# Key and value caches of two heads loaded and worked on as one pair: 64 partitions and 128 rows a head in place of 128 partitions and 64 rows

## The chip, the cores and the metric

The kernel runs on one core of a Trainium2 chip. The metric is the device time of one execution in microseconds (us). TensorE (PE in the profile) does the matrix products, VectorE (DVE) elementwise work and reductions, ScalarE (ACT) the exponentials, GpSimd (POOL) further elementwise work, and SyncE (SP) issues the DMA transfers that bring data from HBM into SBUF.

## The reference

Four layers follow one another on a batch of two single tokens: attention with a cache, a gated MLP, and both again with the same weights and the same caches. All data are float32.

```python
B, Sq, D = 2, 1, 576;  H, Sk, Dh = 32, 8192, 128;  Df = 4608

def _A_ref(x, k_cache, v_cache, wq, wo):              # caches: (B, H, Sk, Dh)
    q = (x @ wq).reshape(B, Sq, H, Dh).transpose(0, 2, 1, 3)
    scores = jnp.einsum("bhqd,bhkd->bhqk", q, k_cache) * (Dh ** -0.5)
    p = _softmax(scores, axis=-1)
    o = jnp.einsum("bhqk,bhkd->bhqd", p, v_cache)
    return o.transpose(0, 2, 1, 3).reshape(B, Sq, H * Dh) @ wo

def _B_ref(x, w_gate, w_up, w_down):
    g, u = x @ w_gate, x @ w_up
    return (_gelu(g) * u) @ w_down

x = A_x
for _ in range(2):
    x = x + _A_ref(_layernorm(x), A_k_cache, A_v_cache, A_wq, A_wo)
    x = x + _B_ref(_layernorm(x), B_w_gate, B_w_up, B_w_down)
```

The keys of one head and one batch entry are 8192 x 128 floats, 4 MiB, and so are its values. There are 64 such heads (32 heads, two batch entries), so one attention reads 512 MiB of caches, and there are two.

## The kernel before

**Caches in SBUF.** A head's 4 MiB lie on 128 partitions: partition p holds 64 consecutive rows of 512 B, so one DMA has 128 runs of 32 KB. A tile called space takes nearly all of SBUF. It is divided into six slots of one head each (8192 floats a partition); the last slot overlaps a ring of four smaller places for weights. A class Arena keeps account, while the program is written, of which stretch is in use and when each slot was last freed. Loads stand in one queue in program order. The head of the queue is written out as a DMA on SP as soon as the account has room for it (pump); whatever frees a stretch calls done, which calls pump. On the chip, SP waits in that same order for the last reader of the room that a load overwrites, and then issues it. So one load that waits holds up all that stand behind it on SP. Most heads load as one transfer (cache); some, at the seams between layers, in quarters of 1 MiB (cache_quarter).

**Order of the loads.** In an attention the keys of head n are followed by the values of head n - 1, then the keys of head n + 1, and so on. At the end of the first attention two key caches and three value caches stay in SBUF. The second attention walks the heads backward and begins with them.

**Work on one head.** For each quarter k of the keys, multiply(n, k) has VectorE multiply the quarter by the query, in place (L461), and GpSimd add the upper half of each product row to the lower half (L465). add_up(n, k) has VectorE sum what is left (L470) and frees the quarter. The query comes broadcast over the partitions from a small matrix product (query, L445). peak and highest find the largest score (L484, L490), softmax takes the exponentials on ScalarE into prz (L496, L499), total makes the sum of the weights (L505, L509). values(n) has TensorE multiply weights and values, 16 products of four rows each (L521), and frees each quarter of the values. gather, context and divide bring the result into place for wo (L537, L546, L551). project multiplies by wo (L563).

**Order of the work.** Each engine works in the order of the program. The steps of neighbouring heads interleave: in the step of head n, the values of head n - 1 are worked on. Two lines of that step matter below:

```python
multiply(n, 0)
if before:
    add_up(n - 1, 3)
    peak(n - 1)
```

The last sum of head n - 1 stands, on VectorE, behind the first multiply of head n. The step then goes on with multiply(n, 1), highest and softmax of n - 1, add_up(n, 0), multiply(n, 2), total, values of n - 1, and the remaining quarters.

**Layers.** plan_attention and plan_mlp queue the loads of both attentions and both MLPs; attention and mlp write the work.

Of the kernel before, what the change touches and what calls it, by code (L numbers as in the profile page):

```python
# [16 lines left out]
B = 2  # L17
# [7 lines left out]
J = SK // P  # L25
NHB = H * B
JC = 16

# [9 lines left out]
SLOT = J * DH  # L38
PART = JC * DH
NSLOT = 6  # L40
# [4 lines left out]
HELD = 5  # L45


class Arena:
# [18 lines left out]
    def slot(self, key, allowed):  # L67

        for s in sorted(allowed, key=lambda s: self.freed[s]):
            if self.clear(s * SLOT, SLOT):  # L70
                return [self.take((key, k), s * SLOT + k * PART, PART) for k in range(4)]
        return None
# [23 lines left out]
def decode_layers(ctx, tc, x_in, kc, vc, wq, wo, wg, wu, wd, out):  # L96
# [36 lines left out]
    def cache_rows(at, hb, src, lo, hi):  # L133

        t = part_at(at, (hi - lo) * DH).rearrange("p (j d) -> p j d", d=DH)
        nc.sync.dma_start(t, src[hb % B, hb // B].rearrange("(p j) d -> p j d", p=P)[:, lo:hi, :])

    def quarter(at):
        return part_at(at, PART).rearrange("p (j d) -> p j d", d=DH)

    def cache(key, src, hb, allowed, pieces=1):

        def make():
            at = arena.slot(key, allowed)
            if at is None:
                return False
            for lo in range(0, J, J // pieces):
                cache_rows(at[0] + lo * DH, hb, src, lo, lo + J // pieces)
            ready[key] = [quarter(a) for a in at]
            places[key] = at  # L150
            return True

        queue.append(make)

    def cache_quarter(key, src, hb, k, where):

        def make():
            if where == "ring":
                at = arena.ring((key, k), PART)
            else:  # L160
                at = arena.take((key, k), places[where][k], PART)
            if at is None:
                return False
            cache_rows(at, hb, src, k * JC, (k + 1) * JC)
            ready.setdefault(key, {})[k] = quarter(at)
            return True

        queue.append(make)
# [58 lines left out]
    def products():  # L227

        def make():
            at = [RING + k * PLACE for k in (2, 3)]  # L230
            if not all(arena.clear(a, PLACE) for a in at):
                return False
            ready["products"] = [quarter(arena.take(("products", k), at[k], PART)) for k in range(2)]
            return True

        queue.append(make)
# [19 lines left out]
    every, front = range(NSLOT), range(HELD)  # L256

    keys_held, values_held = range(NHB - 2, NHB), range(NHB - 3, NHB)

# [3 lines left out]
    def plan_attention(layer, seq):  # L263
        for us in WQ[layer]:

            half_rows(("wq", layer, us[0]), wq, us, None if layer else 3 * SLOT)

        def keys(n):
            hb = seq[n]
            held = hb in keys_held  # L270
            if layer == 1 and held:
                return
            key = ("k", 1 if held else layer, hb)


            if layer and n == 4:
                for turn, k in (("k", 0), ("v", 0), ("v", 1), ("k", 1), ("v", 2), ("v", 3), ("k", 2), ("k", 3)):
                    if turn == "k":
                        cache_quarter(key, kc, hb, k, ("k", 1, seq[1]))
                    else:  # L280
                        cache_quarter(("v", 1, seq[3]), vc, seq[3], k, ("v", 1, seq[0]))
            elif layer and n in (2, 3, 5):
                for k in range(4):
                    cache_quarter(key, kc, hb, k, {2: "ring", 3: ("k", 1, seq[0]), 5: ("v", 1, seq[1])}[n])
            else:

                cache(key, kc, hb, every if layer or n < NHB - 3 else front)

        def vals(n):
            hb = seq[n]  # L290
            held = hb in values_held
            if not (layer == 1 and (held or n == 3)):
                allowed = every if layer or n < NHB - 4 else front
                cache(("v", 1 if held else layer, hb), vc, hb, allowed, 4 if n == NHB - 1 else 1)

        for n in range(NHB + 1):
            if n < NHB - 1:
                keys(n)
            if n == NHB - 2:
                keys(n + 1)  # L300
            if n == NHB:

                if layer == 0:
                    products()
                for g in groups(layer)[:2]:
                    out_rows(layer, g)
            if n > 0:
                vals(n - 1)
        for g in groups(layer)[2:]:
            out_rows(layer, g)  # L310
# [16 lines left out]
    forward = list(range(NHB))  # L327
    backward = forward[::-1]
    plan_attention(0, forward)
    plan_mlp(0)  # L330
    plan_attention(1, backward)
# [6 lines left out]
    ones = consts.tile([P, P], F32, name="ones")  # L338
    nc.vector.memset(ones, 1.0)
# [16 lines left out]
    prz = consts.tile([P, 3, 2 * J + 4], F32, name="prz")  # L356
    nc.vector.memset(prz, 0.0)

# [60 lines left out]
    def attention(layer, seq):  # L419
# [15 lines left out]
        po = psum1.tile([P, GH, B], F32, name="po")  # L435

        oT = once.tile([P, H // GH, GH, 2, B], F32, name="oT", tag="part")

        def query(n):

            h, b = divmod(seq[n], B)
            c, s = (h // 4) % 4, h // 16
            r = s * B + b
            qb[n] = psum2.tile([P, DH], F32, name="qp")
            nc.tensor.matmul(  # L445
                qb[n], pick[32 * c:32 * c + 4, r:r + 1].to_broadcast([4, P]),
                qsb[32 * c:32 * c + 4, (h % 4) * DH:(h % 4 + 1) * DH], start=True, stop=True,
            )

        def multiply(n, k):  # L450

            hb = seq[n]
            held = hb in keys_held
            t = ready["k", 1 if held else layer, hb][k]
            if k == 0:
                S[n] = work.tile([P, J], F32, name="S")
            u = t
            if held and layer == 0:

                u = ready["products"][k % 2]  # L460
# [6 lines left out]
        def add_up(n, k):  # L467
            hb = seq[n]
            held = hb in keys_held
# [3 lines left out]
            if held and layer == 0:  # L473
                if n == NHB - 1 and k >= 2:
                    done(("products", k - 2))
                return
            key = ("k", 1 if held else layer, hb)
            done((key, k))
            if k == J // JC - 1:
                ready.pop(key)  # L480

        def peak(n):
            m = work.tile([P, 1], F32, name="m")
            nc.vector.reduce_max(m, S[n], axis=AX.X)  # L484
# [3 lines left out]
        def highest(n):  # L488
            m1 = work.tile([1, 1], F32, name="m1")
            nc.vector.reduce_max(m1, mT.pop(n), axis=AX.X)  # L490
            mT[n] = psum2.tile([P, 1], F32, name="nb", tag="small")
            nc.tensor.matmul(mT[n], ones[0:1, :], m1, start=True, stop=True)  # L492

        def softmax(n):
            nbs = work.tile([P, 1], F32, name="nbs")
            nc.scalar.mul(nbs, mT.pop(n), -scale)  # L496
            rs[n] = work.tile([P, 1], F32, name="rs")
            pr = prz[:, n % 3, 4:].rearrange("p (g e) -> p g e", e=8)[:, :, 0:4]
            nc.scalar.activation(  # L499
                pr, S.pop(n).rearrange("p (g r) -> p g r", r=4), AF.Exp, bias=nbs, scale=scale, accum_out=rs[n],  # L500
            )

        def total(n):
            tot = psum2.tile([P, 1], F32, name="tot", tag="small")
            nc.tensor.matmul(tot, ones, rs.pop(n), start=True, stop=True)  # L505
            if n % B == 0:
                rinv[n // B] = work.tile([P, B], F32, name="rinv", bufs=4)
            b = seq[n] % B
            nc.vector.reciprocal(rinv[n // B][:, b:b + 1], tot)  # L509

        def values(n):

            hb = seq[n]
            held = hb in values_held
            key = ("v", 1 if held else layer, hb)
            t = ready[key]
            left = not (held and layer == 0)
            for g in range(J // 4):
                c = g % 4
                at = 8 * g + 4 - 4 * (hb % B)  # L520
                nc.tensor.matmul(  # L521
                    acc[32 * c:32 * c + 8, (n // B) % 2, :], prz[:, n % 3, at:at + 8],
                    t[g // 4][:, g % 4 * 4:g % 4 * 4 + 4, :].rearrange("p j d -> p (j d)"),
                    start=(n % B == 0 and g < 4), stop=(n % B == B - 1 and g >= J // 4 - 4),
# [6 lines left out]
        def gather(a):  # L531

            t = osb[a] = work.tile([P, DH], F32, name="osb")
            q = acc[:, a % 2, :].rearrange("p (r d) -> p r d", r=4)
# [6 lines left out]
        def context(a):  # L541

            lo = 32 * (seq[B * a] // B % GH)
            t = osb.pop(a)
# [3 lines left out]
        def divide(a):  # L548
            h = seq[B * a] // B
            lo = 32 * (h % GH)  # L550
            nc.vector.tensor_tensor(  # L551
                out=oT[lo:lo + 32, h // GH, :, :, :],
                in0=po[lo:lo + 32, :, :].unsqueeze(2).to_broadcast([32, GH, 2, B]),
# [184 lines left out]
```

## Time and profile before

| | us |
|---|---|
| median of 3 runs | 2709.51 (2707.89 to 2710.16) |
| the profiled execution | 2710.29 |
| its span, first to last instruction | 2708.4 |
| DVE busy in it | 1889.6 |
| POOL busy | 1208.8 |
| PE busy | 1136.5 |
| ACT busy | 84.7 |

DMA moved 1155.48 MB, a mean of 427 GB/s. Of the 244 whole cache transfers, 122 are keys and 122 values; 28 more have 1 MiB.

How to read the profile: engines are PE (products) and PEld (loading of weights), DVE, ACT, POOL and SP; "SPq" is SP's instruction queue. L461 is line 461 of the kernel. A row of a timeline has start, duration, engine, line, operation, result <- inputs, shapes, count, and in brackets the idle time before it with what ended it. A row of waits has who waited for whom, the total in us, the number of times and the longest. A row of the chain has start, duration and what it was; for a DMA, from its issue to its landing. A row of a window has the stretch, its length, busy time with number of instructions for PE, PEld, DVE, ACT and POOL, the granted clock of TensorE, the busy share of the 16 DMA engines and GB/s.

### The profile page before, as it was taken

The numbers are of one execution on the slowest core, as the hardware profiler recorded it, in microseconds if no ns is written. First come the engines' busy times: TensorE is split into PE (matmuls) and PEld (weight loads), VectorE is DVE, ScalarE is ACT, GpSimd is POOL, SyncE is SP. The second block draws the span as 40 slices with busy tenths as digits, with TensorE's granted clock in tenths as the row PEclk, the third lists the DMA queues.
The fourth block names the chain that finished last, engine by engine and source line by source line (L and its number), as shares of the span: only waits on it lengthen the run. The fifth ranks groups of instructions, "written<-read, shape, count | busy, mean of one in ns | idle before, by whom it ended". The sixth has DMA issues, their size and how long they took to land.

```text
span 2708.4 us, 19293 instructions
## 1 busy us (share of the span) xinstructions
PE 1136.5 (42%) x7320; PEld 401.7 (15%) x7320; DVE 1889.6 (70%) x1807; ACT 84.7 (3%) x399; POOL 1208.8 (45%) x522
## 2 busy tenths in 40 slices
PE   2344434343434344344644434443434343444345
PEld 0111111111111111111211111111111111111122
DVE  5777777777777777776039977777777777777740
ACT  0000000000000000000000000000000000000000
POOL 2545444444544454544016554544444444445420
PEclk8666666666666666666666766566665666666678
DMA  9999999999999999999999999999999999999998
GB/s 418 433 432 430 431 433 432 430 431 432 431 431 431 432 430 432 431 431 421 397 374 419 431 431 431 432 431 430 431 431 432 432 430 430 432 430 432 430 428 378
DMA packets 50379, 1155.48 MB, mean 427 GB/s; under 512 B 5848, under 2 KB 5872, under 8 KB 7408
## 3 DMA queue, kind: packets, MB, share of 16 engines
q1 hardware_dynamic: 50248, 1154.25, 99.6%
q8 instruction: 58, 0.95, 0.1%
q14 instruction: 33, 0.27, 0.0%
q10 hardware_dynamic: 40, 0.01, 0.0%
HBM read 1154.23 MB, written 0.00 MB: 426 GB/s over the span
## 4 chain that ended last, share of the span: by engine, by line
DMA 78%; DVE 11%; PE 8%; issue 2%; POOL 0%; another core or an unknown queue 0%; SPq 0%; ACT 0%; DVEq 0%; POOLq 0%; ACTq 0%
DMA space<-in_A_k_cache_dram 45%; DMA space<-in_A_v_cache_dram 23%; PE acc L521 7%; DVE space L461 6%; DVE S L470 3%; DMA space<-in_A_wo_dram 3%; DMA space<-in_B_w_up_dram 3%; DMA space<-in_B_w_down_dram 2%; DMA space<-in_A_wq_dram 1%; DVE osb L537 1%; PE acc L426 0%; DMA space<-in_B_w_gate_dram 0%; POOL space L465 0%; PE acc L646 0%; DVE m L490 0%
## 5 line engine op out<-in xcount | busy, mean ns | idle before, releaser
L465 POOL TENSOR_TENSOR space<-space 128x1024 f32<-128x1024 f32 x512 | 1205.9, 2356 | 1255.6 <-DVE space L461 1221.6
L461 DVE TENSOR_TENSOR space<-space,qp 128x2048 f32<-128x2048 f32 x512 | 1164.9, 2275 | 479.8 <-DMA space<-in_A_k_cache_dram 457.3
L521 PE MATMUL acc<-space,prz 128*8 128x512 f32 x4096 | 723.8, 870 | 291.8 <-DVE osb L537 170.8
L470 DVE TENSOR_REDUCE S<-space 128x16 f32<-128x1024 f32 x512 | 616.0, 1203 | 3.3 <-POOL space L465 3.3
L486 PE MATMUL mT<-ident,m 128*1 128x128 f32 x128 | 46.9, 366 | 794.1 <-DVE m L484 794.1
L521 PEld LDWEIGHTS acc<-space,prz 128*8 128x8 f32 x4096 | 133.1, 115 | 769.7 <-issue 720.9
L492 PE MATMUL nb<-m,ones 1*128 1x1 f32 x256 | 74.1, 356 | 252.9 <-DVE m L490 252.9
L486 PEld LDWEIGHTS mT<-ident,m 128*1 128x1 f32 x128 | 10.2, 79 | 819.9 <-DVE m L484 813.9
L505 PE MATMUL tot<-rs,ones 128*128 128x1 f32 x256 | 74.6, 361 | 92.8 <-ACT prz L499 92.8
L492 PEld LDWEIGHTS nb<-m,ones 1*128 1x128 f32 x256 | 63.2, 305 | 289.7 <-DVE m L490 289.7
L496 ACT ACTIVATE nbs<-nb 128x1 f32<-128x1 f32 x128 | 21.9, 171 | 2357.8 <-PE nb L492 2357.8
L551 DVE TENSOR_TENSOR oT<-po,rinv 32x16 f32<-32x16 f32 x64 | 10.9, 170 | 112.2 <-PE po L546 112.2
L505 PEld LDWEIGHTS tot<-rs,ones 128*128 128x128 f32 x256 | 63.6, 309 | 104.0 <-ACT prz L499 103.5
L412 POOL TENSOR_TENSOR rstd<-ve,mhalf 128x1 f32<-128x1 f32 x4 | 2.2, 550 | 170.9 <-DVE ve L410 170.9
L445 PE MATMUL qp<-qsb,pick 4*128 4x128 f32 x256 | 62.3, 325 | 28.5 <-DVE space L461 25.4
L537 DVE SCALAR_TENSOR_TENSOR osb<-acc,diag,osb 128x128 f32<-128x128 f32 x192 | 67.3, 351 | 6.8
L671 DVE STREAM_TRANSPOSE o<-o 128x288 f32<-128x288 f32 x4 | 2.8, 691 | 93.1 <-ACT o L669 93.1
L445 PEld LDWEIGHTS qp<-qsb,pick 4*128 4x128 f32 x256 | 38.0, 186 | 88.9 <-PE acc L521 48.1
L416 DVE TENSOR_TENSOR x<-xps,x 128x144 f32<-128x144 f32 x4 | 1.2, 307 | 71.3 <-PE xps L695 41.5
L546 PEld LDWEIGHTS po<-of,osb 128*32 128x32 f32 x512 | 40.1, 152 | 49.4 <-issue 40.8
L499 ACT ACTIVATE prz<-S,nbs 128x64 f32<-128x64 f32 x128 | 44.5, 348 | 4.5 <-ACT nbs L496 0.4
L546 PE MATMUL po<-of,osb 128*32 128x2 f32 x512 | 37.6, 195 | 6.6 <-DVE osb L537 6.6
(56 smaller groups left out, 344.6 us busy)
## 6 DMA issues: line engine op xcount, KB each, us to landing
space<-in_A_k_cache_dram SPq DMA_DIRECT2D x122, 4096.0 KB
space<-in_A_v_cache_dram SPq DMA_DIRECT2D x122, 4096.0 KB
space<-in_A_wo_dram SPq DMA_DIRECT2D x16, 1152.0 KB
space<-in_A_k_cache_dram SPq DMA_DIRECT2D x16, 1024.0 KB
space<-in_A_v_cache_dram SPq DMA_DIRECT2D x12, 1024.0 KB
space<-in_B_w_down_dram SPq DMA_DIRECT2D x9, 1152.0 KB
space<-in_B_w_gate_dram SPq DMA_DIRECT2D x3, 3456.0 KB
space<-in_A_wq_dram SPq DMA_DIRECT2D x3, 3072.0 KB
```

The lines of the kernel that those rows point to most:

```text
L445: nc.tensor.matmul(qb[n], pick[32 * c:32 * c + 4, r:r + 1].to_broadcast([4, P]), qsb[32 * c:32 * c + 4, (h % 4) * DH:(h % 4 + 1) * DH], st ...
L461: nc.vector.tensor_tensor(out=u, in0=t, in1=qb[n].unsqueeze(1).to_broadcast([P, JC, DH]), op=ALU.mult)
L465: nc.gpsimd.tensor_tensor(out=half, in0=half, in1=u[:, :, DH // 2:], op=ALU.add)
L470: nc.vector.tensor_reduce(out=S[n][:, k * JC:(k + 1) * JC], in_=prod.pop((n, k)), axis=AX.X, op=ALU.add)
L486: nc.tensor.transpose(mT[n], m, ident)
L492: nc.tensor.matmul(mT[n], ones[0:1, :], m1, start=True, stop=True)
L496: nc.scalar.mul(nbs, mT.pop(n), -scale)
L499: nc.scalar.activation(pr, S.pop(n).rearrange("p (g r) -> p g r", r=4), AF.Exp, bias=nbs, scale=scale, accum_out=rs[n],)
L505: nc.tensor.matmul(tot, ones, rs.pop(n), start=True, stop=True)
L521: nc.tensor.matmul(acc[32 * c:32 * c + 8, (n // B) % 2, :], prz[:, n % 3, at:at + 8], t[g // 4][:, g % 4 * 4:g % 4 * 4 + 4, :].rearrange(" ...
L537: nc.vector.scalar_tensor_tensor(t, q[:, r, :], diag[:, r:r + 1], t, op0=ALU.mult, op1=ALU.add,)
L546: nc.tensor.matmul(po[lo:lo + 32, i, :], t[:, i::GH], of, start=True, stop=True)
```

## The change

The heads 0 to 29 are taken in pairs: heads h and h + 1 of one batch entry, which lie side by side in HBM, are one item. Head h takes partitions 0 to 63 and head h + 1 partitions 64 to 127, with 128 consecutive rows each: one run of 64 KB a partition, 8 MiB an item, eight parts where a head had four quarters. There are 30 pairs, and four single heads (h = 30 and 31) at the end, laid out as before. A whole pair takes two neighbouring slots of the six.

In the first attention the slots of each load are written out by hand; in the second, pair takes the two neighbouring slots that have been free longest. A few pairs at the seams load in halves or single parts. A pair has two query products, two exponentials and two divisions, since its heads lie on different partitions; value products have the weights of both heads side by side. All eight wo loads of the second attention are queued behind the last values (before, two stood ahead of them). The held caches are those of the same heads as before.

```diff
+class Item:
+    def __init__(self, b, h, heads):
+        self.b, self.h, self.heads = b, h, heads
+        self.rows = SK * heads // P
+        self.parts = self.rows // JC
+
+    def source(self, cache):
+        return cache[self.b, self.h:self.h + self.heads].rearrange("h (q j) d -> (h q) j d", j=self.rows)
+
+ITEMS = [Item(b, h, 2) for h in range(0, H - 2, 2) for b in range(B)]
+PAIRS = len(ITEMS)
+ITEMS += [Item(b, h, 1) for h in range(H - 2, H) for b in range(B)]
...
+    def pair(self, key):
+        for s in sorted(range(0, NSLOT, 2), key=lambda s: max(self.freed[s:s + 2])):
+            at = self.slots(key, (s, s + 1), 8)
+            if at is not None:
+                return at
         return None
...
+    def plan_first():
...
+        for us in WQ[0]:
+            half_rows(("wq", 0, us[0]), wq, us, END - NU * H * DH // 2)
+        last = PAIRS - 1
+        at = [(2 * (i % 3), 2 * (i % 3) + 1) for i in range(2 * PAIRS)]
+        k(0, at[0])
+        for n in range(1, PAIRS):
+            k(n, at[2 * n - 1])
+            v(n - 1, at[2 * n])
+        k(SINGLE[0], (4,))
+        half(("v", 0, last), vc, last, 0, 5)
+        half(("v", 0, last), vc, last, 4, 1)
+        k(SINGLE[1], (3,))
+        v(SINGLE[0], (4,))
+        k(SINGLE[2], (0,))
+        k(SINGLE[3], (2,))
+        v(SINGLE[1], (4,))
+        v(SINGLE[2], (1,))
+        products()
+        for g in groups(0)[:2]:
+            out_rows(0, g)
+        v(SINGLE[3], (3,), (1,) * 4)
...
+    def plan_second():
...
+        for k in range(4):
+            one(("k", 1, last), kc, last, 4 + k, (v62, k))
+        half(("k", 1, last - 1), kc, last - 1, 0, 5)
+        half(("k", 1, last - 1), kc, last - 1, 4, 4)
+        cache(("v", 1, last), vc, last)
+        for n in range(last - 2, -1, -1):
+            cache(("k", 1, n), kc, n)
+            cache(("v", 1, n + 1), vc, n + 1)
+        cache(("v", 1, 0), vc, 0, None, (4, 2, 1, 1))
+        for g in groups(1):
+            out_rows(1, g)
...
         def query(n):
...
+            for i in range(it.heads):
+                h, to = it.h + i, slice(i * HALF, i * HALF + P // it.heads)
...
         def softmax(n):
...
+            for i in range(it.heads):
+                at = slice(i * HALF, i * HALF + P // it.heads)
+                nc.scalar.mul(nbs[at], nb[at, i:i + 1], -scale)
...
+        for i, n in enumerate(seq):
...
+            v = {N - 2: None, N - 1: N - 3}.get(i, i - 1) if layer == 0 else i - 1
...
+            for k in range(ITEMS[n].parts):
+                multiply(n, k)
+                if k == 0 and p is not None:
+                    add_up(p, ITEMS[p].parts - 1)
+                    peak(p)
+                if k == (0 if soon else 1) and p is not None:
+                    highest(p)
+                    softmax(p)
+                if k == 2:
+                    if p is not None:
+                        total(p)
+                    if a is not None:
+                        gather(a)
+                        if p < PAIRS:
+                            context(a)
+                    if v is not None and v >= 0:
+                        values(v)
+                    if a is not None and p >= PAIRS:
+                        context(a)
+                if k > 0:
+                    add_up(n, k - 1)
+                if k == 3 and a is not None:
+                    divide(a)
```

More of the change, by code (lines that the diff above doesn't have):

```diff
@@ L65, in take, with slots @@
         return lo
[L67 to L71, printed above, removed]
+    def slots(self, key, at, parts, first=0):
+        if not all(self.clear(s * SLOT, SLOT) for s in at):
+            return None
+        return [self.take((key, first + k), at[k // 4] * SLOT + k % 4 * PART, PART) for k in range(parts)]
+    def pair(self, key):
[3 more added lines that the diff above has]
+                return at
         return None
@@ L232, in make @@
                 return False
-            ready["products"] = [quarter(arena.take(("products", k), at[k], PART)) for k in range(2)]
+            ready["products"] = [part(arena.take(("products", k), at[k], PART)) for k in range(2)]
             return True
@@ L488, in highest @@
         def highest(n):
[L489 to L492, printed above, removed]
+            heads = ITEMS[n].heads
+            m1 = work.tile([1, 2], F32, name="m1")
+            nc.vector.reduce_max(m1[:, :heads], mT.pop(n).rearrange("p (i q) -> p i q", i=heads), axis=AX.X)
+            mT[n] = psum2.tile([P, 2], F32, name="nb", tag="small")
@@ L516, in values, with accumulator, completes @@
+        of_head = {}
+        def accumulator(n):
+            return acc[:, n % 2 if n < PAIRS else (n - PAIRS) // B, :]
+        def completes(i):
+            return seq[i] < PAIRS or i > 0 and ITEMS[seq[i - 1]].h == ITEMS[seq[i]].h
+        def values(i):
+            n = seq[i]
+            it, key, pr = ITEMS[n], name("v", layer, n), weights_of(n)
             t = ready[key]
-            left = not (held and layer == 0)
-            for g in range(J // 4):
+            left = not (layer == 0 and n in VALUES_HELD)
+            gs = it.rows // 4
+            begins = n < PAIRS or not completes(i)
+            for g in range(gs):
@@ L607, in attention, with finish @@
-        add_up(last, 3)
-        first, second, *others = groups(layer)
-        values(last - 1)
-        peak(last)
-        highest(last)
-        softmax(last)
-        project(first)
-        total(last)
-        gather(H - 2)
-        context(H - 2)
-        divide(H - 2)
-        project(second)
-        values(last)
-        gather(H - 1)
-        context(H - 1)
-        divide(H - 1)
-        for g in others:
+        def finish(n):
+            gather(n)
+            context(n)
+            divide(n)
@@ new lines, in attention @@
+        n, p = seq[-1], seq[-2]
+        add_up(n, ITEMS[n].parts - 1)
+        first, second = groups(layer)[:2]
+        if layer == 0:
+            values(N - 2)
+        peak(n)
+        highest(n)
+        softmax(n)
+        if layer == 0:
+            project(first)
+        total(n)
+        finish(seq[-3] if layer == 0 else p)
+        if layer == 0:
+            project(second)
+        values(N - 1)
+        finish(n)
+        for g in groups(layer)[2:] if layer == 0 else groups(layer):
```

305 lines of the change are left out of this document (144 added, 161 removed).

## The prediction

> **What bounds the kernel now.** I read the page first: shares, traffic by slice, queues, the chain that ended last.
>
> ```profile
> span 2708.4 us, 19293 instructions
> ...
> PE 1136.5 (42%) x7320; PEld 401.7 (15%) x7320; DVE 1889.6 (70%) x1807; ACT 84.7 (3%) x399; POOL 1208.8 (45%) x522
> ...
> GB/s 418 433 432 430 431 433 432 430 431 432 431 431 431 432 430 432 431 431 421 397 374 419 431 431 431 432 431 430 431 431 432 432 430 430 432 430 432 430 428 378
> ...
> q1 hardware_dynamic: 50248, 1154.25, 99.6%
> ...
> DMA 78%; DVE 11%; PE 8%; issue 2%; POOL 0%; another core or an unknown queue 0%; SPq 0%; ACT 0%; DVEq 0%; POOLq 0%; ACTq 0%
> ```
>
> No compute engine is over 70% busy, and SP's one queue holds the 16 DMA engines for 99.6% of the span. The slices of the two attentions run level at 430 to 433 GB/s; only the MLP in the middle and the end dip. Then the stretches by window and the waits.
>
> ```profile
> core 0: us, PE busy (x) PEld busy (x) DVE busy (x) ACT busy (x) POOL busy (x), PEclk, DMA share, GB/s
> 300.00:500.00 200.00, 77.77 (x431) 27.24 (x431) 150.67 (x140) 6.11 (x30) 96.57 (x41) 0.63 1.00 431
> ...
> 1350.00:1370.00 20.00, 10.51 (x212) 5.65 (x216) 1.84 (x7) 0.97 (x3) 0.00 (x0) 0.81 1.01 420
> ...
> 1700.00:2500.00 800.00, 326.65 (x1767) 112.92 (x1767) 598.78 (x555) 25.10 (x123) 386.29 (x164) 0.63 1.00 431
> ```
> ```profile
> DVE space L461 <- DMA space<-in_A_k_cache_dram: 457.3, 115, 14.2
> ```
>
> The DMA share in either attention is 1.00, while DVE stands still 457.3 us for keys. So the time is bytes over rate plus the time in which the DMA queue is empty, and that is next to nothing today. The bytes do not change. The change can therefore act in two ways: on the rate, and on whether the queue always has a transfer waiting.
>
> **The change, first the rate.** In layer 0, 30 key and 29 value pairs move whole as 8 MiB; in layer 1, 28 and 29: 116 transfers. Each replaces two of 4 MiB, and its 128 runs of 64 KB replace 256 of 32 KB. At 431 GB/s an engine gets 26.9 GB/s, and a 32 KB run takes 1216 ns. The 1350 to 1370 row is w_down with runs of 9 KB, engines as busy, at 420: 351 ns for 9216 B. A line through both gives about 12 ns fixed per run. Each engine saves 116 x 128 / 16 = 928 such costs: 11 us. If the engine cuts 64 KB into two, nothing is saved but some completion marks; and since both rates are rounded, I take 9 us and keep 0 to 12. On the other side, the two heads of a pair lie 4 MiB apart and neighbouring partitions 64 KB: no row shows a rate at such a spacing, so a loss is not excluded (a rival below).
>
> [...]
>
> **Then the queue in layer 0.** This is the term that decides. The room for caches becomes three places of 8 MiB, and layer 0 writes the places out by hand: load number i goes to place i mod 3, in the order K0, K1, V0, K2, V1, K3, V2 ... So V(n) overwrites K(n), and the load directly ahead of V(n) in the queue is K(n+1). When is K(n) done with? Its last part's add_up stands, in DVE's order, behind the first multiply of item n+1, which waits for K(n+1) to land. That order exists already, and the timeline shows it:
>
> ```profile
> 298.74 2.29 DVE L461 TENSOR_TENSOR space<-space,qp 128x2048 f32<-128x2048 f32 x1 [2.35 <-DMA space<-in_A_k_cache_dram]
> 300.94 1.21 DVE L470 TENSOR_REDUCE S<-space 128x16 f32<-128x1024 f32 x1
> ...
> 302.18 0.33 SPq L136 DMA_DIRECT2D space<-in_A_v_cache_dram  x1
> ```
> ```profile
> 302.18 45.11 DMA space<-in_A_v_cache_dram
> ```
> ```profile
> SPq L136 <- DVE m L484: 799.1, 122, 19.3
> ```
>
> The multiply starts as the keys land, the previous item's sum follows, and 302.18 - 298.74 = 3.44 us after the landing SP issues the next load. SP's wait list has this release 122 times. Today it costs nothing: with six places the transfer issued at 302.18 lands 45.11 us later, so over four transfers of 9.73 us lie in the queue. After the change nothing lies there: K(n+1) has landed, V(n) is the head of SP's queue and waits, and K(n+2) waits behind it in order. The DMA engines stand still from the landing until V(n)'s first bytes, in every pair.
>
> The price of one such stop. The 3.44 us are sure. After the issue there is a restart, which this profile shows where layer 1 begins with an empty queue:
>
> ```profile
> 1409.38 14.62 SPq L136 DMA_DIRECT2D space<-in_A_k_cache_dram  x5
> ```
> ```profile
> 1409.00:1410.00 1.00, 0.00 (x0) 0.00 (x0) 1.00 (x2) 0.00 (x0) 1.00 (x1) 0.50 0.00 0
> 1410.00:1411.00 1.00, 0.00 (x0) 0.00 (x0) 1.00 (x1) 0.00 (x0) 0.41 (x1) 0.50 0.86 139
> 1411.00:1412.00 1.00, 0.00 (x0) 0.00 (x0) 1.00 (x2) 0.00 (x0) 0.37 (x1) 0.50 0.81 319
> ```
>
> Against 431 GB/s that loses 0.62 us before 1410, 0.68 in the next us and 0.26 in the one after: 1.6 us from issue to full rate. Ahead of the 3.44 us is a landing's own lag, from the engines' last bytes to the waiting instruction. The end of the kernel bounds it:
>
> ```profile
> 2704.00:2705.00 1.00, 0.61 (x16) 0.33 (x16) 0.00 (x0) 0.00 (x0) 0.00 (x0) 1.00 0.08 30
> 2705.00:2705.50 0.50, 0.46 (x12) 0.11 (x8) 0.00 (x0) 0.00 (x0) 0.00 (x0) 1.00 0.00 0
> ```
> ```profile
> 2705.11 0.47 PE xps L695 x8
> ```
> ```profile
> 2705.94 0.64 SPq L708 DMA_DIRECT2D out_dram<-x  x2
> ```
>
> The engines are nearly all idle by 2704.1, and the matmul on the last w_down piece starts at 2705.11: a lag between 0.1 and 1.0 us; I take 0.5. One stop is 3.44 + 1.6 + 0.5 = 5.5 us. The low end is 5.0. For the high end I take issue to end of the last store, 2708.4 - 2705.94 = 2.46 us, in place of 1.6, and the whole lag: 6.9.
>
> How many: V1 to V28 in layer 0 (V0 finds a free place; V29 goes in two halves to places freed earlier, with 9.7 us of another transfer in front). Among the singles, V of the first takes the place of its own K, directly behind K of the second: one more. 29 x 5.5 = 160 us (146 to 200).
>
> **Layer 1** lets the allocator choose, so I walked the frees. There V takes the place of the V before it, and K that of the K two before, freed 3.4 us after the next K has landed, with a value transfer of 19.5 us then in flight. One head's value products take up to 6.6 us in the chain, a pair's some 13, beside 19.5 us of the next keys:
>
> ```profile
> 660.25 6.59 PE acc L521 x32
> ```
>
> So nothing drains there; 6.5 us are to spare, less the restart. At the layer's start the loads are as before, down to the quarters; then two halves of a pair come where two 4 MiB loads came. The first whole V pair needs the place that the values of item 3 free:
>
> ```profile
> 1424.16 2.03 SPq L136 DMA_DIRECT2D space<-in_A_v_cache_dram  x2
> ...
> 1430.38 13.20 SPq L136 DMA_DIRECT2D space<-in_A_k_cache_dram  x6
> 1447.51 0.33 SPq L136 DMA_DIRECT2D space<-in_A_v_cache_dram  x1
> 1460.17 0.33 SPq L136 DMA_DIRECT2D space<-in_A_k_cache_dram  x1
> ```
> ```profile
> 1468.72 5.08 PE L521 MATMUL acc<-space,prz 128*8 128x512 f32 x32
> ```
>
> It can issue at 1468.72 + 5.08 = 1473.8. Ahead of it stand the last of the five key quarters, eleven more of 1 MiB from 1424.16 on, and two halves of 4 MiB at 1447.51 and 1460.17: 20 MiB or 48.7 us, which from a start at about 1425 are through at 1473.7. I price one stop at its restart, 2 us (0 to 5).
>
> **The rest costs nothing.** The two query products, two exponentials, two divisions and larger reductions lie on engines that wait. A pair's DVE work is at most two of today's heads:
>
> ```profile
> 1433.71 0.22 DVE L484 TENSOR_REDUCE m<-S 128x1 f32<-128x64 f32 x1
> ...
> 1464.23 0.22 DVE L484 TENSOR_REDUCE m<-S 128x1 f32<-128x64 f32 x1
> ```
>
> That is 30.5 us against 38.9 of loads. If the additions took 8 us of DVE per pair, this cover would be gone. The first pair lands 9.7 us later than the first head; that is absorbed in the same slack. wq lies elsewhere, but its matmuls end before the 19.5 us of K0. Layer 1's two early wo groups move behind V; the queue only changes order.
>
> **Sum.** 160 + 2 - 9 = 153 us. The profiled execution took 2710.29 us (its span 2708.4 and 1.9 around), 0.8 above the median of 2709.51; on the median 2862 us.
>
> **Rivals.** A: the queue never empties, because V(n) is released before K(n+1) lands. Then only the rate acts: 2709.5 + 2 - 9 = 2702 us, faster. For it speaks that DVE needs only 30.5 of 38.9 us; it decides by whether K(n)'s last sum can run before K(n+1) lands. Against it stands the order in the rows above. 5%.
>
> B: layer 1 drains too, if its allocator hands V the place of K. 28 more stops of 5.5: 3016 us. It would need the values to be freed later than K, that is over 19.5 us after they land, against 13. 3%.
>
> C: the new spacing slows the transfers. At 420 in place of 431, the lowest busy rate of the rows here, 116 x 19.5 us grow by 2.6%, 59 us, and the 9 are not won: 2930 us. 5%. [...]
>
> [...] 1%.
>
> E: the stops are there but shorter than the 0.2% that this kernel's measurement can tell (some 5 us); they would have to be 0.4 us each, against 3.44 of DVE work alone. 1%.
>
> My forecast, stops in layer 0 only, has the remaining 85%.
>
> **Range.** 29 stops of 5.0 with the full 12 us won give 2843; 29 of 6.9 with 5 us more at layer 1's start and nothing won give 2715 + 200 = 2915, whose corner is unlikely; 2840 to 2905 holds some 82%. Slower has 85 + 3 + 5 = 93%, faster 6%, same 1%.
>
> **What would show it.** In layer 0's windows the DMA share falls to 38.9 / 44.4 = 0.88 and the rate to some 378 GB/s, in layer 1 it stays at 1.00 and 431 to 434. The timeline shows SP issuing each V 3.4 us after the first multiply of the next item, and V landing some 21 us after its issue instead of 45; DVE's first multiplies come 44.4 us apart in layer 0 and 38.9 in layer 1. The forecast is wrong if layer 0 keeps a share of 1.00, if V is issued before the multiply, or if layer 1 falls as well. The packet count tells whether 64 KB goes as one: 14,848 fewer data packets than with halves.

## The result, and the profile after

| | us |
|---|---|
| changed kernel, median of 5 runs | 2894.69 (2893.45 to 2896.13) |
| kernel before, beside it, median of 5 runs | 2709.85 (2707.89 to 2711.1) |
| ratio, 95% interval | 1.0682 (1.0667 to 1.0698) |
| the profiled execution's span | 2891.7 |

The change makes the kernel 185 us slower. The forecast was 2862 us, 153 us slower, with a range from 2840 to 2905.

The page of the changed kernel, its lines in the order in which those of before were shown:

```profile
span 2891.7 us, 18050 instructions
...
PE 900.5 (31%) x7020; PEld 295.4 (10%) x7020; DVE 1872.4 (65%) x1688; ACT 90.1 (3%) x399; POOL 1209.8 (42%) x528
...
GB/s 421 392 363 349 381 359 392 349 377 377 336 404 349 392 348 357 397 348 390 388 420 412 387 430 432 430 435 433 432 434 435 431 433 434 432 433 435 434 422 380
...
q1 hardware_dynamic: 33400, 1154.24, 93.4%
...
DMA 80%; PE 10%; DVE 8%; issue 1%; POOL 1%; SPq 0%; ACT 0%; ACTq 0%; DVEq 0%; POOLq 0%
```

The bytes are the same, 1154.2 MB, but the queue holds the DMA engines for 93.4% of the span instead of 99.6%. The slices split in two: the first 19 (layer 0) lie between 336 and 421 GB/s, those of layer 1, but for its start and the end of the kernel, between 430 and 435, where before both layers were level at 430 to 433. The windows say the same, the DMA share and GB/s in the last two columns:

```profile
100.00:1300.00 1200.00, 310.49 (x2119) 98.67 (x2119) 762.75 (x663) 35.45 (x162) 496.14 (x211) 0.59 0.86 367
1700.00:2500.00 800.00, 239.64 (x1645) 74.38 (x1649) 603.04 (x524) 27.59 (x126) 393.90 (x168) 0.61 1.00 433
```

In layer 1 the share is still 1.00, at 433 GB/s against 431 before. In layer 0 the engines stand idle for 14% of the time. DVE's wait for keys has grown from 457.3 us in 115 waits to 758.9 in 59, and SP waits 1741.1 us for the release by an item's last sum (the reduction named here follows it):

```profile
DVE space L512 <- DMA space<-in_A_k_cache_dram: 758.9, 59, 23.8
```
```profile
SPq L166 <- DVE m L533: 1741.1, 63, 45.7
```

One landing of keys in layer 0, in the timeline and in the chain:

```profile
240.53 2.29 DVE L512 TENSOR_TENSOR space<-space,qp 128x2048 f32<-128x2048 f32 x1 [17.12 <-DMA space<-in_A_k_cache_dram]
242.74 1.21 DVE L519 TENSOR_REDUCE S<-space 128x16 f32<-128x1024 f32 x1
...
243.98 0.33 SPq L166 DMA_DIRECT2D space<-in_A_v_cache_dram  x1
...
244.40 0.38 SPq L166 DMA_DIRECT2D space<-in_A_k_cache_dram  x1
```
```profile
244.40 42.24 DMA space<-in_A_k_cache_dram
...
286.66 2.29 DVE space L512
```

After 17.12 us of waiting the first multiply of K(n+1) starts at 240.53; the sum of the item before it follows; SP issues V(n) at 243.98, 3.45 us after the landing, and K(n+2) right behind it at 244.40. That K lands 42.24 us later, and the next item begins at 286.66. Two transfers of 8 MiB at 433 GB/s take 38.7 us, so of the 46.1 us from one landing to the next 7.4 are lost in this item (6.8 on average, as worked out below). This is the stop that was forecast. The packet records of the trace (start, duration and size of every piece that a DMA engine moved) hold 29 gaps of 4.7 to 4.9 us in layer 0 in which no DMA engine moves a byte of SP's queue, one for each of the 29 places counted.

### The profile page after: what moved, and what is told of

The parts are those of the page before. It is cut to its first block, busy times and chain, and to the rows that moved or that the text cites. A ratio compares the mean times of both kernels' runs of the same rounds, so it can differ in the third digit from the quotient of the medians.

```text
span 2891.7 us, 18050 instructions
## 1 busy us (share of the span) xinstructions
PE 900.5 (31%) x7020; PEld 295.4 (10%) x7020; DVE 1872.4 (65%) x1688; ACT 90.1 (3%) x399; POOL 1209.8 (42%) x528
## 3 DMA queue, kind: packets, MB, share of 16 engines
q1 hardware_dynamic: 33400, 1154.24, 93.4%
## 4 chain that ended last, share of the span: by engine, by line
DMA 80%; PE 10%; DVE 8%; issue 1%; POOL 1%; SPq 0%; ACT 0%; ACTq 0%; DVEq 0%; POOLq 0%
DMA space<-in_A_k_cache_dram 44%; DMA space<-in_A_v_cache_dram 29%; PE acc L605 9%; DVE space L512 5%; DVE S L519 3%; DMA space<-in_B_w_up_dram 3%; DMA space<-in_A_wo_dram 2%; DMA space<-in_B_w_down_dram 2%; DMA space<-in_A_wq_dram 1%; POOL space L516 0%; DVE m L533 0%; PE acc L743 0%; DMA space<-in_B_w_gate_dram 0%; DMA x<-in_A_x_dram 0%; PE xps L792 0%
## 5 line engine op out<-in xcount | busy, mean ns | idle before, releaser
L512 DVE TENSOR_TENSOR space<-space,qp 128x2048 f32<-128x2048 f32 x512 | 1166.2, 2278 | 781.0 <-DMA space<-in_A_k_cache_dram 758.9
L605 PE MATMUL acc<-space,prz 128*8 128x512 f32 x4096 | 598.4, 748 | 630.7 <-DMA space<-in_A_v_cache_dram 625.8
L519 DVE TENSOR_REDUCE S<-space 128x16 f32<-128x1024 f32 x512 | 619.3, 1210 | 3.3 <-POOL space L516 3.3
L535 PE MATMUL mT<-ident,m 128*1 128x128 f32 x68 | 24.9, 367 | 815.8 <-DVE m L533 815.8
L543 PE MATMUL nb<-m,unit 1*128 1x2 f32 (+1 forms) x136 | 39.2, 355 | 126.6 <-DVE m L541 126.6
L575 PE MATMUL tot<-sums,unit 128*128 128x2 f32 x120 | 35.2, 363 | 92.2 <-ACT prz L566 92.2
L500 PE MATMUL qp<-qsb,pick 4*64 4x128 f32 (+1 forms) x256 | 30.4, 302 | 79.3 <-DVE space L512 76.0
L566 ACT ACTIVATE prz<-S,nbs 64x128 f32<-64x128 f32 (+1 forms) x128 | 50.7, 396 | 12.5 <-POOL prz L556 8.5
L543 PEld LDWEIGHTS nb<-m,unit 1*128 1x128 f32 x136 | 33.3, 303 | 147.9 <-DVE m L541 147.9
L575 PEld LDWEIGHTS tot<-sums,unit 128*128 128x128 f32 x120 | 30.0, 310 | 97.3 <-ACT prz L566 97.3
L792 PE MATMUL xps<-space,hT 128*4 128x144 f32 x576 | 29.7, 373 | 20.8 <-DMA space<-in_B_w_down_dram 19.2
L743 PE MATMUL acc<-space,xt 128*8 128x288 f32 x288 | 28.8, 536 | 19.9 <-DMA space<-in_B_w_up_dram 10.8
```

Source lines behind the costliest of these rows:

```text
L500: nc.tensor.matmul(qb[n][to, :], pick[32 * c:32 * c + 4, r:r + 1].to_broadcast([4, P // it.heads]), qsb[32 * c:32 * c + 4, (h % 4) * DH:(h ...
L512: nc.vector.tensor_tensor(out=u, in0=t, in1=qb[n].unsqueeze(1).to_broadcast([P, JC, DH]), op=ALU.mult)
L519: nc.vector.tensor_reduce(out=S[n][:, k * JC:(k + 1) * JC], in_=prod.pop((n, k)), axis=AX.X, op=ALU.add)
L535: nc.tensor.transpose(mT[n], m, ident)
L543: nc.tensor.matmul(mT[n][:, :heads], ones[0:1, :], m1[:, :heads], start=True, stop=True)
L566: nc.scalar.activation(pr[at, lo:].rearrange("p (g e) -> p g e", e=4)[:, 0:it.rows // 2:2, :], s[at, :it.rows].rearrange("p (g r) -> p g r ...
```

## The experiments

The theory: the 29 stops are the whole slowdown. From 24 landings, the first multiplies at 240.53 and at 1333.25, an item in layer 0 takes 45.5 us, which leaves 6.8 per stop; 29 of them are some 197 us (198 in the expectations below), from which the rate gives some 13 back. Rivals: pairs load slowly in layer 0 for another reason; the hand-written places are bad in themselves; the stop is a latency of the transfers and not the order on VectorE.

**Places alone.** Even keys, odd keys and values each keep a place of their own, so V overwrites V as in layer 1:

```diff
-        at = [(2 * (i % 3), 2 * (i % 3) + 1) for i in range(2 * PAIRS)]
+        at = [(0, 1), (4, 5)]
...
-            k(n, at[2 * n - 1])
-            v(n - 1, at[2 * n])
-        k(SINGLE[0], (4,))
-        half(("v", 0, last), vc, last, 0, 5)
-        half(("v", 0, last), vc, last, 4, 1)
+            k(n, at[n % 2])
+            v(n - 1, (2, 3))
+        k(SINGLE[0], (0,))
+        half(("v", 0, last), vc, last, 0, 1)
+        half(("v", 0, last), vc, last, 4, 5)
```

> Places alone: keys of even pairs, keys of odd pairs and values each keep a place of 8 MiB of their own in layer 0, so the values overwrite the values before them. Theory (29 stops of the queue, about 6.8 us each, less 13 us won on the rate): no stop is left, DMA share 1.00 in layer 0 as in layer 1, 2894.7 - 198 = 2697 us. Rival (pairs load slowly in layer 0, whatever the order): layer 0 stays near 370 GB/s and the time above 2880 us.

Measured: 2702.1 us, 0.9971 (0.9960 to 0.9983) of the kernel before. Its windows in layer 0 and layer 1, and a K load in its chain:

```profile
200.00:1100.00 900.00, 275.72 (x1891) 84.00 (x1895) 670.70 (x580) 30.20 (x138) 437.92 (x186) 0.61 1.00 433
1700.00:2450.00 750.00, 221.07 (x1540) 68.25 (x1540) 554.01 (x479) 24.95 (x114) 360.68 (x153) 0.61 1.00 433
```
```profile
611.87 35.29 DMA space<-in_A_k_cache_dram
```

Both layers now have a share of 1.00, and a K load lands 35.29 us after its issue, of which its own bytes take 19.4: when it was issued, the transfer ahead of it was still under way. The pairs, their work and their transfers are as in the changed kernel; only places differ. So 2894.7 - 2702.1 = 192.6 us are the stops, 6.6 us each, and everything else in the change together makes the kernel 0.3% faster. The forecast of 2697 us was missed by 5: the stops cost 193 us and not 198. The rival by which pairs load slowly in layer 0 is out.

**The sum first.** The places of the changed kernel stay; in layer 0 the last sum moves ahead of the next multiply:

```diff
+                if k == 0 and p is not None and layer == 0:
+                    add_up(p, ITEMS[p].parts - 1)
+                    peak(p)
                 multiply(n, k)
-                if k == 0 and p is not None:
+                if k == 0 and p is not None and layer == 1:
```

> The places of the changed kernel, but in layer 0 the last sum of an item stands ahead of the first multiply of the next on VectorE. Theory: K(n) is released some 31 us after it landed, 8 us before K(n+1) lands, so the stops go without touching the places: 2697 us, at most 2705. Rival (the places are bad in themselves, by address or by neighbours): as the changed kernel, 2895 us.

Measured: 2701.91 us, ratio 0.9974 (0.9964 to 0.9985). Layer 0 in its windows:

```profile
100.00:600.00 500.00, 150.44 (x1053) 48.03 (x1053) 378.06 (x325) 17.08 (x78) 244.58 (x105) 0.61 1.00 431
600.00:1100.00 500.00, 147.10 (x1013) 47.05 (x1013) 373.95 (x323) 17.08 (x78) 240.67 (x104) 0.61 1.00 433
```

The same places without the order give no stop, so the rival by which the places are bad in themselves is out. It takes both, the place and the order, and either alone is harmless.

**The sum later.** For the pairs of layer 0 it moves behind the second multiply:

```diff
-                if k == 0 and p is not None:
+                if k == (1 if layer == 0 and n < PAIRS else 0) and p is not None:
                     add_up(p, ITEMS[p].parts - 1)
```

> The places of the changed kernel, and for the pairs of layer 0 the last sum of an item stands one multiply later on VectorE (behind the second). Theory: each of 28 stops grows by one multiply, 2.2 us: 2894.7 + 62 = 2957 us. Rival (the stop is set by something other than this sum, for example by the transfer's own latency): 2895 us.

Measured: 2956.36 us, ratio 1.0909 (1.0892 to 1.0925): 61.7 us over the changed kernel, 2.2 us for each of 28 stops. Its timeline and its window of layer 0:

```profile
295.99 4.49 DVE L512 TENSOR_TENSOR space<-space,qp 128x2048 f32<-128x2048 f32 x2 [18.61 <-DMA space<-in_A_k_cache_dram]
...
300.40 1.21 DVE L519 TENSOR_REDUCE S<-space 128x16 f32<-128x1024 f32 x1
301.64 0.33 SPq L166 DMA_DIRECT2D space<-in_A_v_cache_dram  x1
```
```profile
100.00:1300.00 1200.00, 298.22 (x2025) 93.39 (x2025) 725.05 (x626) 32.81 (x150) 469.19 (x200) 0.58 0.82 350
```

SP issues V 5.65 us after the landing, where it was 3.45. The 2.2 us of VectorE work put in front of the release cost 2.2 us per pair: in layer 0 this work had become part of the critical path. The rival by which the transfer's own latency alone sets the stop is out.

**Halves.** Places and order as changed, but the pairs of layer 0 load in two transfers:

```diff
-        k(0, at[0])
+        k(0, at[0], (4, 4))
...
-            k(n, at[2 * n - 1])
-            v(n - 1, at[2 * n])
+            k(n, at[2 * n - 1], (4, 4))
+            v(n - 1, at[2 * n], (4, 4))
```

> The places and the order of the changed kernel, but pairs of layer 0 load as two transfers of 4 MiB (parts 0 to 3, then 4 to 7; runs of 32 KB). Theory: the first multiply waits for the first half only, the sum and the release then lie beside the second half, which takes 9.7 us against 5 to 7 us of stop, so the stops go: 2697 us plus the lost half of the gain on runs, some 2704 us. Rival (places bad in themselves): 2895 us.

Measured: 2710.68 us, ratio 1.0008 (0.9999 to 1.0017), 7 us over the forecast. The windows show where those are:

```profile
100.00:1200.00 1100.00, 384.63 (x2288) 111.88 (x2292) 816.58 (x711) 38.07 (x174) 532.04 (x226) 0.63 1.00 431
1200.00:1240.00 40.00, 15.73 (x106) 4.96 (x97) 17.77 (x21) 0.61 (x3) 11.90 (x6) 0.69 0.80 339
```

28 stops are gone, since the release now falls beside the second half of K(n+1). The 29th, among the singles, which still load whole, stands there: 20% of 40 us. The expectation had left it out. From the 2702.1 us measured above, this stop (6.6 us) and the 32 KB runs of layer 0 (half of what the next experiment finds, some 3) make 2712.

**Run length.** On the kernel with places of its own, whole pairs load in two transfers with runs of 32 KB, and then in four with runs of 16 KB:

```diff
-            for m in pieces or (parts,):
+            for m in pieces or (4,) * (parts // 4):      # 32 KB; (2,) * (parts // 2) for 16 KB
```

> As the kernel with places of their own for even keys, odd keys and values, but whole pairs load as two transfers of 4 MiB with runs of 32 KB in both layers. Theory (longer runs and fewer transfers save 0.23 us in 38.95 per pair of loads, by the durations of single packets): 13 us slower than with 64 KB runs, about 2710 us, like the kernel before. Rival (run length does nothing; the rate is set by bytes alone): 2697 us, the same.

Measured: 2707.56 us, ratio 0.9995 (0.9986 to 1.0004): about half of the step that the theory forecast.

> The kernel with places of their own, with whole pairs loaded in quarters of 2 MiB with runs of 16 KB in both layers. Theory (a fixed cost per run and per transfer, from 432.5 GB/s at 64 KB and 430.9 at 32 KB): twice the step from 64 to 32 KB is lost again, the steady rate is near 428 GB/s and the time some 2720 us. Rival (the step between 64 and 32 KB was no cost per run): 431 GB/s and 2707 us, as with 32 KB.

Measured: 2725.35 us, ratio 1.0058 (1.0045 to 1.0071), 5 us over the forecast. The kernel with 64 KB, once more beside it:

> The kernel with places of their own once more, unchanged, beside the other three on one chip: 2702 us, within 3.

Measured: 2700.98 us, ratio 0.9971 (0.9961 to 0.9982). The windows of layer 1 with 32 KB and with 16 KB:

```profile
1700.00:2450.00 750.00, 267.08 (x1544) 73.76 (x1544) 556.90 (x484) 26.22 (x120) 362.47 (x154) 0.62 1.00 431
```
```profile
1700.00:2450.00 750.00, 264.84 (x1541) 65.08 (x1539) 549.86 (x476) 24.94 (x114) 357.99 (x152) 0.64 1.01 428
```

433, 431 and 428 GB/s: by the packet records 432.5, 430.9 and 427.6, or 9.70, 9.73 and 9.81 us for 4 MiB. Halving the run costs 0.036 us and then 0.075, twice as much for twice as many more, as a fixed cost does: in 4 MiB an engine has 4 more runs and half a completion mark more, then 8 and one, some 8 ns for each. The step from 64 to 32 KB was forecast at 13 us and came out at some 6.5 in the times, and at 8.4 by 0.036 us for each of 232 halves. The 13 was worked out from the durations of single packets, and those of 32 KB overlap a little: in the window of layer 1 they add up to 1.002 of the time, those of 64 KB to 1.000. That accounts for 13 against 8.4; the 2 us from there to 6.5 stay open. The step from 32 to 16 KB is 17.8 us in the times and 17.4 by the rates. Which part of it belongs to the run and which to the transfer was not told apart; the next experiment was meant to.

**One transfer per head.** 4 MiB transfers that keep runs of 64 KB:

```diff
+        if hi - lo == 8:
+            for i in range(2):
+                nc.sync.dma_start(t[i * HALF:(i + 1) * HALF], rows[i * HALF:(i + 1) * HALF])
```

> As the kernel with places of their own, but each whole pair loads as two transfers of 4 MiB, one per head, 64 partitions with runs of 64 KB each. Theory (the run length counts, the size of the transfer does not): within 3 us of 2697 us, if 64 partitions are spread over all 16 engines. Rival 1 (transfer size counts): 2705 to 2710 us. [...]

Measured: 5125.74 us, ratio 1.8928 (1.8902 to 1.8954). A window of its layer 0:

```profile
300.00:800.00 500.00, 75.89 (x510) 23.08 (x514) 173.50 (x150) 7.87 (x36) 112.75 (x49) 0.55 1.00 208
```

Neither expected time is near. All sixteen engines are busy, share 1.00, at 208 GB/s, and a 64 KB packet takes 5.1 us in place of 2.4. So a transfer into partitions 0 to 63 alone, and then one into 64 to 127, runs at less than half the rate, 208 GB/s against the 433 of the kernel with places of its own; what halves it was not shown. As for run or transfer, the experiment tells nothing.

**Instruction fetches.** Landing to landing in layer 0 takes either some 44.7 or some 46.0 us. Queue 8 of the profile carries instructions, 55 packets of 16 KB or 0.90 MB, which is 64 B for each of TensorE's 14,040 matmuls and weight loads; before, 0.95 MB is 65 B for each of 14,640. So I take it for TensorE's. In the packet records, the 17 intervals between stops in which a packet of queue 8 falls take 46.0 us on average, with a standard deviation of 0.2; the 10 without take 44.7, with 0.3. In the 17 the last engine finishes 0.5 to 1.9 us after the next to last (median 1.4), in the 10 at most 0.7 us after it; with an empty queue behind it, all wait. To test whether fetches do this, 150 tiny instructions per pair were added to idle ScalarE:

```diff
                     softmax(p)
+                    if layer == 0 and n < PAIRS:
+                        for _ in range(150):
+                            nc.scalar.mul(spare, spare, 1.0)
```

> The changed kernel with 150 further tiny ScalarE instructions per pair in layer 0 (about 4350 in all, some 17 more fetches of instructions by DMA), on an engine that stands idle for over 40 us per pair. Theory (a fetch delays one of the 16 DMA engines by about 1.5 us, and where the queue runs empty the landing waits for that engine): layer 0's stops grow on average by some 0.6 us each, 2895 + 10 to 25 = 2905 to 2920 us. Rival (the spread between the engines has another cause): 2895 us, within 3.

Measured on the changed kernel: 2896.86 us, ratio 1.0696 (1.0682 to 1.0711): 2 us more, where the theory asked for 10 to 25 and the rival for at most 3.

> The kernel with places of their own with the same 150 further ScalarE instructions per pair. Theory: the queue never runs empty, a late engine is made up for by the next transfer, and 17 fetches of 1 us on one of 16 engines cost about 1 us in all: within 3 us of the kernel without them, about 2697 us. Rival (fetches cost time wherever they fall, or the instructions hold up work): as much slower as the other kernel with extra instructions.

Measured on the kernel with places of its own: 2720.39 us, ratio 1.0043 (1.0029 to 1.0056); 18 us more, where the theory asked for at most 3 and the rival for as much as on the other kernel; neither is met. Its windows of layer 0:

```profile
100.00:600.00 500.00, 145.73 (x1001) 45.56 (x1005) 368.86 (x321) 406.05 (x1996) 238.62 (x102) 0.60 1.00 431
600.00:1100.00 500.00, 146.90 (x1035) 45.20 (x1026) 361.42 (x312) 400.18 (x1968) 236.67 (x101) 0.62 0.99 424
1100.00:1300.00 200.00, 77.52 (x585) 27.08 (x585) 143.40 (x139) 98.15 (x482) 90.80 (x43) 0.64 0.98 417
```

The rate holds at first and falls later. The 33 more fetches (63 packets of queue 14, against 30) came as packets of 8 KB. In the trace each transfer ends with sixteen signals, which I take for one from each engine as it is done. By their times, the last engine is 0.3 us behind the middle of the sixteen at the start, falls further behind to 8.5 us at 540 us, and then stays between 7.6 and 9.6 us to 1210 us; without the extra instructions it is never over 4. So the late engine was not made up for by the transfers that followed. The reading is that each engine has a sixteenth of every transfer to move, that a late one may lag as far as loads are issued ahead, and that its pace is everyone's from then on. If so, a deeper queue only puts the bill off:

```diff
                 softmax(n - 1)
+                if layer == 0 and n < NHB - 4:
+                    for _ in range(75):
+                        nc.scalar.mul(spare, spare, 1.0)
```

> The kernel before with 75 further tiny ScalarE instructions per head in layer 0 (about 4400 in all, as in the two other kernels with extra instructions). Theory (ScalarE's instruction fetches all fall on one of the 16 DMA engines, which must still move its sixteenth of the bytes, so its lag adds up, whatever the lead of the queue): some 18 us more than the kernel before, 2727 us. Rival (a deep queue, 45 us ahead, hides it): within 3 us of 2709.

Measured: 2728.22 us, ratio 1.0071 (1.0057 to 1.0084), 20 us more. Its windows, and then the same two stretches of the kernel before:

```profile
600.00:1100.00 500.00, 197.41 (x1079) 68.49 (x1079) 368.62 (x342) 396.42 (x1968) 236.11 (x101) 0.64 1.00 431
1100.00:1300.00 200.00, 86.06 (x519) 29.36 (x519) 145.26 (x138) 98.82 (x491) 93.82 (x40) 0.63 0.95 404
1300.00:1400.00 100.00, 59.40 (x788) 23.50 (x788) 9.50 (x36) 1.93 (x6) 0.56 (x1) 0.69 0.93 376
```
```profile
1100.00:1300.00 200.00, 87.93 (x680) 34.29 (x684) 135.19 (x133) 6.12 (x30) 84.78 (x36) 0.65 1.00 424
1300.00:1400.00 100.00, 60.25 (x664) 19.07 (x660) 8.53 (x32) 1.94 (x6) 1.10 (x2) 0.69 0.99 403
```

With a queue 45 us deep, layer 0 still runs at 431 GB/s up to 1100 us, and the lag is paid at the seam, where the MLP needs all of its data: 404 for 424, and 376 for 403 GB/s. The signals show the lag itself: it grows steadily, from 0.4 us at the start to 23 us at 1245 us, where the kernel before has 4. These 19 us are about the 20 that were lost. So two kernels show that ScalarE's fetches cost some 0.6 us each (18 us over 33, 20 over 35).

Why did they cost so little in the changed kernel? Its trace with the extra instructions answers by the same grouping. The 10 intervals in which only queue 14 fetches take 45.1 us on average, against 44.6 in the 8 of the changed kernel in which neither queue does. The 17 in which queue 8 fetches as well take 46.0 us, as they did without the extra instructions. At a stop everyone waits for the latest engine, and where TensorE's fetch has made one late already, another late engine added nothing. That TensorE's fetches are what makes the stops uneven rests on this grouping; no run took them away.

**The short stop at layer 1's start.** The first whole V pair there loads in halves, each when its slot is free:

```diff
-        cache(("v", 1, last), vc, last)
+        half(("v", 1, last), vc, last, 0, 2)
+        half(("v", 1, last), vc, last, 4, 3)
```

> The kernel with places of their own, and the first whole value pair of layer 1 loads as two halves of 4 MiB, each issued when its own slot comes free. Theory (the short stop at layer 1's start comes from that pair's wait for both slots): 2 us less than without, about 2700 us, and the third gap of layer 1's start gone. Rival (the engines are late there for another reason): no change, 2702 us.

Measured: 2697.9 us, ratio 0.9960 (0.9948 to 0.9973), and its packet records have no gap near 1470 us, the third gap. But in two executions of the kernel without this edit that gap was 0.9 and 0.2 us, and the 3 us against 2700.98 for places alone lie within the overlap of the two intervals, so the gain of this last step is not settled.

## Why the prediction was right

**The mechanism and its count held.** V(n) waits for K(n)'s last sum, this waits behind a multiply for K(n+1), and nothing else is queued. Taking away the place or the order takes the stops away, and delaying the sum by 2.2 us lengthens each by 2.2. The 3.44 us from the first multiply to the issue came out as 3.45.

**The term that was too small is the price of a stop**: 5.5 us forecast, 6.6 measured; 29 times 1.1 is the 32 us by which the forecast fell short. It held three parts, and the packet records of 28 stops size each of them:

| part of a stop, us | forecast | mean measured |
|---|---|---|
| last bytes to the first multiply | 0.5 | 0.37 |
| first multiply to SP's issue | 3.44 | 3.44 |
| restart: issue to first bytes, and what the first packet of each engine takes over 2.42 | 1.6 | 0.95 + 0.65 |
| engines idle before the last bytes of the landing | none | 1.2 |
| sum | 5.5 | 6.6 |

The step that failed is the landing's lag. It was taken as the time from the last bytes to the waiting instruction, and its 0.5 us would have covered that. But the sixteen engines do not finish together: on average an engine stands idle for 1.2 us (0.2 to 1.9) before the last one is done, and for this the sum had no term. In layer 1, with a transfer always waiting, the share of 1.00 shows that this spread costs nothing. The row at the end of the kernel from which the lag was read counts packets where they start: "nearly all idle by 2704.1" is too early for the last engine, whose bytes came in at 2704.6, 0.5 us ahead of the matmul. The low bound of the stops, 29 x 5.0, is 145 us and not 146. The upper bound, 6.9 us, held.

**The rate** won about what was forecast: 9 us in the sum, and 6.5 in the times or 8.4 by the steady rates; with the stops away the whole change is 0.29% under the kernel before, 7.9 us. The runs of 64 KB go as one packet each: SP's queue has 33,400 packets in the kernel with 64 KB and 50,104 in the one with 32 KB. The difference of 16,704 is the 14,848 data packets forecast and 16 completion marks for each of 116 transfers.

**Layer 1** has a share of 1.00, so the walk of its allocator was right, and rival B is out; rival C is out with 433 GB/s; rival A is what the kernel with places of its own does, at 2702.1 us for 2702 worked out. In steady flow one transfer of 8 MiB gains 0.07 us over two of 4 MiB, so fewer transfers alone had little to win. **The rest at nothing**, the doubled queries, exponentials and divisions, held too: the share of 1.00 would not stand otherwise. The 2 us put at layer 1's start are not settled: the gap there is 0.3 us in the changed kernel's trace, and its cost is too small for the times to tell.

In the windows, layer 0 was forecast at a share of 0.88 and 378 GB/s and has 0.86 and 367; landings were to be 44.4 us apart and are 45.5.

## What to carry to other kernels

When fewer, larger buffers hold the same bytes, look for the load that overwrites the buffer whose last reader waits, in its own engine's program order, for the load just ahead in the queue: here the queue ran empty at that load, 29 times. The larger transfers won some 8 us and the stops cost 193. Two cures each turned 6.8% slower into 0.3% faster: give each stream its own buffers, or run the last reader before the instruction that waits. Loading in halves took the stops away as well, but gave up the gain on runs. A stop cost more than latency plus work, since the drained queue also paid for the slowest of its engines: 1.2 of 6.6 us.

## What the runs showed of the hardware

- Transfers to 64 neighbouring partitions, one after the other, kept all engines busy at 208 GB/s, against 433 with 128.
- After a stop, the first bytes came 0.95 us after SP's issue, and the first 64 KB packet of each engine took 3.07 us in place of 2.42 (means of 28 stops).
- In these two kernels bound by DMA, instructions on an idle engine were not free: some 4400 on ScalarE cost 18 and 20 us, with 33 and 35 more fetches and one DMA engine that fell behind, by 9 and 23 us. A queue 45 us deep delayed this cost and did not remove it: 431 GB/s up to 1100 us, then 404 and 376 where the kernel without the instructions had 424 and 403.
- The rate of large transfers still depended a little on the run: 428, 431 and 433 GB/s with 16, 32 and 64 KB.
